# Where the spectra of modes 56 to 59 are made, and when the first output unit is prepared, in a fused attention and spectral-mixing kernel

## The chip, the cores and the metric

The kernel runs on one core of one Trainium2 chip. A core has five engines with instruction queues of their own: TensorE (PE, with its weight loads PEld), VectorE (DVE), ScalarE (ACT), GpSimd (POOL) and SyncE (SP). All of them work on on-chip memory (SBUF, and PSUM for the results of matmuls); 16 DMA engines move data. In this kernel SP issues the hardware-queued DMAs and POOL the software-queued ones. The metric is the device time of one execution in microseconds (us), as the median of several runs.

## The reference

There are two stages. The first is causal attention in a window of 128 tokens with a linear bias, for 8 batches, 8 heads, 576 tokens and 64 values a head. Its output, with the heads side by side, is `x`, of 8 x 576 x 512. The second mixes in frequency:

```
X = np.fft.rfft(x, axis=1)
Xr, Xi = (np.real(X[:, :n_modes]), np.imag(X[:, :n_modes]))
Yr = np.einsum('bmd,mde->bme', Xr, w_r) - np.einsum('bmd,mde->bme', Xi, w_i)
Yi = np.einsum('bmd,mde->bme', Xr, w_i) + np.einsum('bmd,mde->bme', Xi, w_r)
Y[:, :n_modes] = Yr + 1j * Yi
y = np.fft.irfft(Y, n=S, axis=1)
u = x + y
return (u + np.maximum(u @ w_ch, 0.0)).astype(np.float32)
```

There are 64 modes, and each has a real and an imaginary weight matrix of 512 x 512 in FP32, 1 MiB each: 127 of the 128 are needed (the imaginary part of mode 0 is not), 133 MB in all. The output is 9.44 MB.

## The kernel before

**Stages.** Attention runs until about 135 us of the span and leaves `x` in SBUF and the forward spectra of all batches in `XC`. Then comes the weight stage, until about 410 us, and then the output stage.

**The weight stage** (the loop over `g` at line 821) takes the weight matrices as 128 tiles in a fixed order, eight to a group of four modes: group `g` has modes 4g to 4g + 3, and `LAST` is 15. Within a group, `i` counts the places 0 to 7, and tile number `k` is 8g + i. In groups 0 to 14 two tiles are worked on together (at even `i`); in group 15 they come one by one, so that tile 120 is at `i` = 0 and tile 127 at `i` = 7. Four matmuls of 128x512 a tile (line 847) add it into `acc`, in which each mode of the group has 32 rows: 16 for the real parts of the batches and 16 for the imaginary ones. In group 15 the first three modes (60 to 62) are added into a second accumulator, `part_acc`.

Each tile is one DMA of 1 MiB that SP issues (line 465), once the tile whose buffer it takes is used up; some earlier ones are cast on the way, and POOL issues those. The last tile, 127, is loaded in three parts.

**Between the tiles** PE gets one piece of other work per `i`: first what stands in `quads` (a generator per group, resumed once per place), else the next entry of `side`, else a `warm()`: three matmuls of 128x512 whose result isn't used (line 664).

**From an accumulator to spectra.** `quad_end` scales `acc` into `yq` (DVE), transposes it (four PE transposes) and puts the result into `YT`, where the modes of 32 consecutive places (half `hf` 0 or 1) come together for each pair of batches (two DVE copies). When the 32 modes of a half are there, `spectra(hf, bp)` makes for the batch pair `bp`: four matmuls of 128x128 into `z`, which turn `YT` back into rows (one row for each batch, mode and real or imaginary part), and four of 128x512 with the channel weights `wch` into `zw`. ACT casts `zw` into `ZW[:, bp, hf]`, DVE `z` into `Z[:, bp, hf]`. The four blocks of half 0 are put into `side` after group 7. The four of half 1 (modes 32 to 63) are put there after group 13 and run in group 14, at `i` = 1 to 4: modes 56 to 63 are zero in `YT` then (line 541), and their rows in `Z` and `ZW` are filled later.

**The late modes.** `late_end` does this for group 14 (modes 56 to 59) and for the first three modes of group 15. It scales the accumulator into `yq` and has POOL copy the eight rows (six for the part) of each batch into `Z`, one DMA for each batch (`patch`, line 624): eight DMAs of 8 KB for group 14; six of 6 KB for the part, since batches 0 and 1 aren't copied there. It then transposes `yq`. For group 14 it also multiplies by `wch` (`late_channels`), casts on ACT, and has POOL copy the rows of each batch into `ZW`: eight more DMAs of 8 KB. Mode 63 is done after the loop (lines 911 to 946), and then the channel rows of the whole group 15.

**Output units.** There are 18 `units`, each of 64 or 128 tokens of two batches. During groups 8 to 14, `side` makes for each unit `project` (tokens times `wch`, plus half 0 from `ZW`, kept in `XW`) and `augment` (half 0 from `Z`, added into `x`). What is left for the output stage is half 1: a unit needs four small matmuls to bring `XW` into PSUM (`restore`, line 738), four with `ZW` (`spread`, line 635), and as many with `x` and `Z`. ACT then applies ReLU (line 778), DVE adds (line 802) and SP stores (lines 804, 811). For the first unit this is started inside the weight loop: at `i` = 7 of group 15, ahead of tile 127's matmuls, the pool `ps` of the weight stage is closed, the pool `head` is opened on its PSUM banks, and `begin(0)`, `channels(0)`, `take(0)`, `add_tokens(0)` and `finish_tokens(0)` issue 16 matmuls of 64x512. Units 0 and 1 take the modes 60 to 63 of batches 0 and 1 straight from `yq` and `yw`, through the table `FM` (`last_rows`, line 762).

**What sets the order.** The program runs in the order in which it is written (`manual_schedule`): each engine takes its own instructions in that order and waits by semaphores for what other engines and DMAs make. PSUM has eight banks of 128 x 512 FP32.

Of the kernel before, what the change touches and what calls it, by code (L numbers as in the profile page):

```python
# [10 lines left out]
FP32 = mybir.dt.float32  # L11
BF16 = mybir.dt.bfloat16
# [8 lines left out]
P = 128  # L21
# [378 lines left out]
def kernel(  # L400
# [10 lines left out]
    nc = tc.nc  # L411
    ctx.enter_context(tc.manual_schedule(engines=ALL | {SP}))
    B, H, S, _ = q.shape
    NM, DM, _ = moe_w_r.shape
# [3 lines left out]
    HM = NM // 2  # L418
# [21 lines left out]
    LAST = NM // 4 - 1  # L440
    turns = []
# [26 lines left out]
    with ExitStack() as actx:  # L468
        at = _Attention(tc, actx, q, k, v, (ident, F, FT), x, XC, raw)
        n = len(at.units)  # L470
# [67 lines left out]
    with ExitStack() as mctx:  # L538
        fix = mctx.enter_context(tc.tile_pool(name="fix", bufs=1))
        YT = fix.tile([P, 2, 4, B, HM, 2], BF16, name="YT")  # L540
        nc.gpsimd.memset(YT[:, 1, :, :, HM - 8 :], 0.0)
        pool = mctx.enter_context(tc.tile_pool(name="fin", bufs=2))
        wctx = mctx.enter_context(ExitStack())
        wpool = wctx.enter_context(tc.tile_pool(name="w", bufs=NWA, reuse_waits="tile"))
# [4 lines left out]
        ps = pctx.enter_context(tc.tile_pool(name="fps", bufs=1, space=PSUM))  # L549
        heads, free, idle = {}, [], []  # L550

        def late_end(acc, g, n):

            rows = slice(0, 32 * n)
            yq = pool.tile([P, DM], BF16, tag="yq", bufs=3)
            nc.vector.tensor_scalar_mul(yq[rows], acc[rows], 2.0 / S)
            patch([(nc.gpsimd, b) for b in range(2 if g == LAST else 0, B)],
                  yq, g, lambda b: Z[:, b // 2, 1], 0, 2 * n)
            yield
            tr = lps.tile([P, 4, P], BF16, tag="tr", name="tr")  # L560
            for et in range(4):
                nc.tensor.transpose(tr[:, et, rows], yq[rows, et * P : (et + 1) * P],
                                    ident[rows, rows])
            yT = pool.tile([P, 2, 4, P], BF16, tag="xT", name="xT")[:, 0]
            nc.vector.tensor_copy(yT[:, :, rows], tr[:, :, rows])
            heads[g] = yq, yT
            if n < 4:
                return
            yield
            zw = ps.tile([P, DM], FP32, tag="zw", bufs=1, name="zw")  # L570
            yw = pool.tile([P, DM], BF16, tag="yq", bufs=3)
            late_channels(zw, yT, yw, slice(0, DM))
            patch([(nc.gpsimd, b) for b in range(B)], yw, g, lambda b: ZW[:, b // 2, 1])

        def late_channels(zw, yT, yw, c):
            for et in range(4):
# [40 lines left out]
            zw = ps.tile([P, DM], FP32, tag="zw", bufs=1, name="zw")  # L617
            spectra(hf, bp, z, zw)

        def patch(todo, rows, g, dst, lo=0, hi=8):  # L620

            for queue, b in todo:
                r = 64 * (b % 2) + 8 * (g % 8)
                queue.dma_start(out=dst(b)[r + lo : r + hi],  # L624
                                in_=rows.rearrange("(k v) e -> k v e", v=16)[lo:hi, b])

# [190 lines left out]
        quads, side, recycle = [], [], list(again)  # L817
        ZW = Z = XW = FM = FC = pairs = wch = w2 = None
        K1 = spot[again[-1]]
        turn = iter(turns)  # L820
        for g in range(NM // 4):
            if g == 0:
                lps.tile([P, 2, 4, P], BF16, tag="tr", name="tr")
            acc = (lps if g % 2 else ps).tile([P, DM], FP32, tag="acc", bufs=1, name="acc")
            if g == LAST:
                part_acc = ps.tile([P, DM], FP32, tag="z", bufs=1, name="z")
            for i in range(8):
                k = 8 * g + i
                if i == 7 and g == LAST:
                    pctx.close()  # L830
                    head = mctx.enter_context(
                        tc.tile_pool(name="hps", bufs=1, space=PSUM, reuse_waits="tile"))
                    heads.update(mm=[head], yy=[head])
                    idle.append(0)
                    free.append(0)
                    begin(0)
                    channels(0)
                    take(0)
                    add_tokens(0)
                    finish_tokens(0)  # L840
                now = next(turn) if g == LAST or i % 2 == 0 else []
                for a in range(4):
                    for t in now:
                        m, ri = t // 2, t % 2
                        c0 = (a // 2 * 2 * NC + 16 * (1 - ri) + a % 2 * 8) * NM + m
                        into = part_acc if g == LAST and m < NM - 1 else acc
                        nc.tensor.matmul(  # L847
                            into[32 * (m % 4) : 32 * (m % 4) + 32],
                            lhsT=XC[:, c0 : c0 + 31 * NM + 1 : NM], rhs=wq[t][a],
                            start=(ri == 0 and a == 0), stop=(ri == (m > 0) and a == 3),  # L850
                            tile_position=(0, 32 * (m % 4)),
                        )
                own = next((t for t in homes if spot[t] == k), None)
                if own is None:
                    continue
                if recycle:
                    load_w(1, early, True, [recycle.pop(0)])
                elif homes[own] not in (early, None):
                    load_w(1, homes[own], False)
                if k == K1:  # L860
                    actx1.close()
                    w2 = mctx.enter_context(
                        tc.tile_pool(name="w2", bufs=NWB, side="right", reuse_waits="tile")
                    )
                    load_w(NWB, w2, False)
                    right = mctx.enter_context(
                        tc.tile_pool(name="late", bufs=1, side="right", reuse_waits="tile")
                    )
                    wch = right.tile([P, 4, DM], BF16, name="wch")
                    nc.gpsimd.dma_start(out=wch, in_=moe_w_ch.rearrange("(a p) e -> p a e", p=P))  # L870
                    ZW = right.tile([P, B // 2, 2, DM], BF16, name="ZW")
                    Z = right.tile([P, B // 2, 2, DM], BF16, name="Z")
                    XW = right.tile([P, len(units), 2, DM], BF16, name="XW")
                    FM = right.tile([P, 2, 2 * P], BF16, name="FM")
                    nc.gpsimd.memset(FM, 0.0)
                    for b in range(2):
                        nc.gpsimd.dma_start(
                            out=FM.rearrange("(k v) b s -> k v b s", v=16)[:, b, b],
                            in_=FT[64 * b + 56 : 64 * b + 64, b, : 2 * P],
                        )  # L880
                    FC = right.tile([P, P], BF16, name="FC")
                    pairs = right.tile([P, P], BF16, name="pairs")
                    nc.gpsimd.memset(FC, 0.0)
                    for i, rows in enumerate((slice(0, 64), slice(64, P))):
                        nc.gpsimd.tensor_copy(FC[rows, i::2], FT[rows, i, FULL * P :])
                        nc.gpsimd.tensor_copy(pairs[:, i::2], ident[:, rows])

                if quads:
                    if next(quads[0], True):
                        quads.pop(0)  # L890
                elif side and (i != 3 or g > LAST - 4):
                    side.pop(0)()
                elif g > LAST - 2 and k < 2 * NM - 1 or g == LAST - 2 and not side:
                    warm()
                if g == LAST and i == 5:
                    quads.append(late_end(part_acc, g, 3))
                    next(quads[0])
            if g < LAST:
                quads.append((late_end(acc, g, 4) if g == LAST - 1 else quad_end(acc, g)))
                next(quads[0])  # L900
            if g == 7:
                side += [partial(stream_spectra, 0, bp) for bp in range(B // 2)]
                for j in range(len(units)):
                    side += [partial(project, j), *([partial(augment, j - 1)] if j else [])]
                side.append(partial(augment, len(units) - 1))
            elif g == LAST - 2:
                side = [partial(stream_spectra, 1, bp) for bp in range(B // 2)] + side
        wctx.close()
        heads["out"] = mctx.enter_context(tc.tile_pool(name="res", bufs=6, reuse_waits="tile"))

# [8 lines left out]
        for i, c in enumerate(sides):  # L919
            nc.scalar.mul(yq[96:, c], acc[96:, c], 2.0 / S)  # L920
            for et in (2 * i, 2 * i + 1):
# [1 line left out]
                                    ident[96:, 96:])  # L923
            nc.vector.tensor_copy(yT[:, 2 * i : 2 * i + 2, 96:],
                                  trs[i][:, 2 * i : 2 * i + 2, 96:])
        patch([(nc.sync, 0), (nc.sync, 1)], yq, LAST, lambda b: Z[:, b // 2, 1])
        patch([(nc.sync, 2)] + [(nc.gpsimd, b) for b in (3, 4, 5, 6)], yq, LAST, lambda b: Z[:, b // 2, 1], 6)
        yw = F[:, : DM // (2 * NM)].rearrange("p a b -> p (a b)")
        for i, c in enumerate(sides):
            zl = zps.tile([P, DM], FP32, tag=f"z{i}", name=f"zl{i}")  # L930
# [10 lines left out]
        take(1)  # L941
        begin(1)
        channels(1)
        channel_rows = partial(patch, rows=yw, g=LAST, dst=lambda b: ZW[:, b // 2, 1])
        channel_rows([(nc.sync, 0), (nc.sync, 1)] + [(nc.gpsimd, b) for b in range(2, B)])
        patch([(nc.gpsimd, 7)], yq, LAST, lambda b: Z[:, b // 2, 1], 6)

        assert not side
        for j in (0, 1):
# [37 lines left out]
```

## Time and profile before

| | us |
|---|---|
| three runs | 445.92, 446.85, 446.88; median 446.85 |
| the profiled execution, whole time | 446.24 |
| its span, first to last instruction | 444.1 |
| busy in the span: PE / DVE / ACT / POOL | 329.6 / 184.4 / 162.6 / 59.5 |
| tile 120's matmuls start | 391.53 |
| tile 127's matmuls start | 409.66 |
| first matmul behind the loop (line 915) | 410.70 |
| first store issued | 415.37 |

Times inside the execution are counted from the start of the span. A line of the timeline has the start, the duration from the first to the last of the instructions that it merges, the engine, the line of the program, the operation, what it writes and reads, the shape and the number of instructions; in brackets stands how long the engine sat idle before it, and what ended that ("issue" is time in which it waited for nothing that the profile shows). SP's DMA issues are shown as SPq. A line of the table of stretches has the stretch, its length, the busy time of each engine in it, the granted TensorE clock (1.00 is full, 0.50 half), the busy share of the DMA engines, and what they moved.

### The profile page before, as it was taken

How to read it: one execution, taken by the hardware profiler on the slowest of the kernel's cores; microseconds unless marked ns; L12 is line 12 of the kernel's file. 1: busy time of each engine (PE TensorE's matmuls, PEld its weight loads, DVE VectorE, ACT ScalarE, POOL GpSimd, SP SyncE). 2: the span in 40 equal slices, each digit the busy share in tenths (PEclk: the TensorE clock that was granted, in tenths of full speed). 3: DMA queues.
4: the chain of work that ended last, by engine and by line, in shares of the span. 5: the costliest groups of instructions: out<-in, count | busy, mean ns of one | idle time of the engine just before them, and what ended most of it. 6: DMA issues, size and time to landing. Idle time of an engine off the chain costs nothing. (4 is left out here: it accounts for less than half of the span.)

```text
span 444.1 us, 8410 instructions
## 1 busy us (share of the span) xinstructions
PE 329.6 (74%) x3488; PEld 180.2 (41%) x3510; DVE 184.4 (42%) x331; ACT 162.6 (37%) x212; POOL 59.5 (13%) x123
## 2 busy tenths in 40 slices
PE   5579899979886554444455498998989998876982
PEld 3367677757664311111111133443444444332430
DVE  7789899987863201010000122232223322310684
ACT  6849899968860000000000012222222222210780
POOL 8611010101303100200000000000000000054500
PEclk9969999989998855555555579999999999999997
DMA  8999999999999999999999999999999999997598
GB/s 279 313 321 295 298 320 294 320 290 302 220 217 320 314 319 313 337 384 427 419 422 422 420 423 419 418 423 418 421 418 421 419 420 421 422 405 267 178 378 307
DMA packets 53721, 157.05 MB, mean 354 GB/s; under 512 B 5156, under 2 KB 24372, under 8 KB 41268
## 3 DMA queue, kind: packets, MB, share of 16 engines
q1 hardware_dynamic: 47860, 140.56, 82.0%
q0 software_dynamic: 5824, 15.97, 18.2%
q8 instruction: 27, 0.44, 0.4%
q14 instruction: 10, 0.08, 0.0%
HBM read 162.53 MB, written 9.44 MB: 387 GB/s over the span
## 5 line engine op out<-in xcount | busy, mean ns | idle before, releaser
L847 PE MATMUL acc<-w,XC 128*32 128x512 bf16 x456 | 92.7, 497 | 61.2 <-DMA w<-in_moe_w_r_dram 33.3
L847 PEld LDWEIGHTS <-XC 128*32 128x32 bf16 x508 | 39.5, 148 | 115.4 <-issue 101.7
L294 ACT ACTIVATE att<-sc 128x1024 bf16<-128x1024 f32 x64 | 64.1, 1032 | 10.2 <-PE sc L284 10.2
L612 ACT CAST ZW<-zw 128x512 bf16<-128x512 f32 x8 | 4.7, 586 | 134.6 <-PE zw L610 134.6
L331 PE MATMUL av<-vb,att 128*128 128x132 bf16 (+1 forms) x576 | 38.7, 218 | 10.9 <-DVE x L347 5.3
L331 PEld LDWEIGHTS <-att 128*128 128x128 bf16 x704 | 36.8, 99 | 16.3 <-DVE x L347 9.7
L678 PE MATMUL my<-wch,xT 128*64 128x512 bf16 x288 | 34.5, 381 | 5.8 <-ACT x L709 4.3
L584 DVE TENSOR_SCALAR yq<-acc 128x512 bf16<-128x512 f32 x13 | 8.9, 687 | 71.7 <-PE acc L847 71.7
L687 ACT CAST XW<-my 128x512 bf16<-128x512 f32 x36 | 19.3, 589 | 51.5 <-PE my L635 51.5
L624 POOL DMA_DIRECT2D Z<-yq x19 | 9.7, 519 | 209.2 <-issue 203.0
L659 DVE COPY xT<-tr 128x1024 bf16<-128x1024 bf16 x18 | 12.5, 692 | 55.6 <-PE tr L657 55.6
L256 ACT COPY qkT<-tp 128x1152 bf16<-128x1152 bf16 x30 | 33.5, 1116 | 2.8 <-PE tp L250 2.3
L284 PE MATMUL sc<-qkT 64*64 64x256 bf16 (+2 forms) x640 | 25.1, 263 | 4.9 <-ACT qkT L256 1.2
L347 DVE TENSOR_TENSOR x<-av,rec 128x640 bf16<-128x640 f32 x32 | 26.4, 824 | 1.1
L678 PEld LDWEIGHTS <-xT 128*64 128x64 bf16 x288 | 17.2, 109 | 21.7 <-issue 9.3
L802 DVE TENSOR_TENSOR o<-yy,r 128x1024 f32<-128x1024 f32 (+1 forms) x22 | 21.5, 1025 | 4.7 <-ACT r L778 3.0
L233 DVE CAST vb<-vr 64x1024 bf16<-64x1024 f32 x32 | 22.6, 708 | 0.6 <-DMA vr<-in_v_dram 0.4
L710 DVE CAST x<-my 128x512 bf16<-128x512 f32 x18 | 12.5, 692 | 24.6 <-PE my L635 24.6
L709 ACT CAST x<-my 128x512 bf16<-128x512 f32 x18 | 10.6, 586 | 32.3 <-PE my L635 32.3
L284 PEld LDWEIGHTS <-qkT 64*64 64x64 bf16 x640 | 14.5, 109 | 19.1 <-issue 16.1
L305 DVE TENSOR_TENSOR att<-att,mask 128x1024 bf16<-128x1024 bf16 x32 | 20.6, 684 | 0.0
L778 ACT ACTIVATE r<-mm 128x1024 f32<-128x1024 f32 (+1 forms) x22 | 17.9, 874 | 4.7 <-PE mm L748 2.5
(134 smaller groups left out, 401.2 us busy)
## 6 DMA issues: line engine op xcount, KB each, us to landing
w<-in_moe_w_i_dram SPq DMA_DIRECT2D x49, 1024.0 KB, 17.9
w<-in_moe_w_r_dram SPq DMA_DIRECT2D x48, 1024.0 KB, 16.4
qr<-in_q_dram SPq DMA_DIRECT2D x16, 576.0 KB, 9.3
kr<-in_k_dram SPq DMA_DIRECT2D x16, 576.0 KB, 8.0
vr<-in_v_dram SPq DMA_DIRECT2D x64, 128.0 KB, 7.6
out_dram<-o SPq DMA_DIRECT2D x13, 512.0 KB, 4.6
w<-in_moe_w_r_dram POOLq DMA_DIRECT2D x12, 512.0 KB, 8.9
w<-in_moe_w_i_dram POOLq DMA_DIRECT2D x10, 512.0 KB, 8.6
```

The source lines that it names most:

```text
L233: nc.vector.tensor_copy(self.vb[u % 2][row, :, :, :, W * half : W * half + D], src[row, :2])
L256: (self.nc.vector.tensor_copy if u < 2 and w == "q" else self.nc.scalar.copy)(dst.rearrange("q h (p j) -> q h p j", j=TPP), tp.rearrange(" ...
L284: nc.tensor.matmul(sc[64 * half : 64 * half + 64, e, j * 256 + c0 : j * 256 + c0 + n], lhsT=qkT[row, 1, h, k0 + j : k0 + P : 2], rhs=qkT[r ...
L294: self.nc.scalar.activation(self.att[u % 2][:, kt * 8 * P : (kt + 1) * 8 * P], sc.rearrange("p e n -> p (e n)"), AF.Exp, scale=1.0 / math. ...
L305: nc.vector.tensor_tensor(out=rows, in0=rows, in1=self.table[:, heads], op=ALU.mult)
L331: nc.tensor.matmul(bank[:, qt * W : qt * W + rhs[j].shape[1]], lhsT=att[:, o : o + P], rhs=rhs[j], start=(n == 0 and j == 0), stop=(n == l ...
L347: nc.vector.tensor_tensor(out=self.x[:, b, :, cs].rearrange("p t (h d) -> p h t d", h=2), in0=tiles[:, :, :, :D], in1=rec.unsqueeze(-1).br ...
L678: nc.tensor.matmul(mm[ROWS[half]], lhsT=lhsT, rhs=wch[:, dt], start=(dt == 0), stop=False, skip_group_check=True,)
L687: nc.scalar.copy(XW[:, j, n], mms[n])
L778: nc.scalar.activation(r[:, c], mm[:, c], AF.Relu)
L802: nc.vector.tensor_tensor(out=o[:, c], in0=yy[:, c], in1=r[:, c], op=ALU.add)
L847: nc.tensor.matmul(into[32 * (m % 4) : 32 * (m % 4) + 32], lhsT=XC[:, c0 : c0 + 31 * NM + 1 : NM], rhs=wq[t][a], start=(ri == 0 and a == 0 ...
```

## The change

Group 14 (modes 56 to 59) ends with `quad_end` like every group before it, so its rows reach `Z` and `ZW` through `YT` and `spectra`. Only modes 60 to 63 are zero in `YT`. The four `spectra` blocks of half 1 are therefore put into `side` one group later, after group 14, and run in group 15 at `i` = 1 to 4, behind the matmuls of tiles 121 to 124, where `late_channels` and fillers stood. In group 14 their places go to the two entries of `side` that are left, and to fillers. The branch for four modes in `late_end` is gone, with its sixteen row copies. Since `z` and `part_acc` now live at the same time, `part_acc` has a PSUM bank of its own. The first unit's 16 matmuls, with the closing and opening of the pools, are issued at `i` = 6, ahead of tile 126's matmuls, instead of at `i` = 7. The new way in which `now` is found gives the same tiles at the same places.

```diff
-        nc.gpsimd.memset(YT[:, 1, :, :, HM - 8 :], 0.0)
+        nc.gpsimd.memset(YT[:, 1, :, :, HM - 4 :], 0.0)
...
-        def late_end(acc, g, n):
-
-            rows = slice(0, 32 * n)
+        def late_end(acc):
+
+            rows = slice(0, 96)
             yq = pool.tile([P, DM], BF16, tag="yq", bufs=3)
             nc.vector.tensor_scalar_mul(yq[rows], acc[rows], 2.0 / S)
-            patch([(nc.gpsimd, b) for b in range(2 if g == LAST else 0, B)],
-                  yq, g, lambda b: Z[:, b // 2, 1], 0, 2 * n)
+            patch([(nc.gpsimd, b) for b in range(2, B)], yq, lambda b: Z[:, b // 2, 1], 0, 6)
             yield
...
-            heads[g] = yq, yT
-            if n < 4:
-                return
-            yield
-            zw = ps.tile([P, DM], FP32, tag="zw", bufs=1, name="zw")
-            yw = pool.tile([P, DM], BF16, tag="yq", bufs=3)
-            late_channels(zw, yT, yw, slice(0, DM))
-            patch([(nc.gpsimd, b) for b in range(B)], yw, g, lambda b: ZW[:, b // 2, 1])
+            heads[LAST] = yq, yT
...
             if g == LAST:
-                part_acc = ps.tile([P, DM], FP32, tag="z", bufs=1, name="z")
+                part_acc = ps.tile([P, DM], FP32, tag="pa", bufs=1, name="pa")
             for i in range(8):
                 k = 8 * g + i
-                if i == 7 and g == LAST:
+                if i == 6 and g == LAST:
                     pctx.close()
...
-                now = next(turn) if g == LAST or i % 2 == 0 else []
+                now = turns.pop(0) if turns and spot[turns[0][0]] == k else []
...
                 if g == LAST and i == 5:
-                    quads.append(late_end(part_acc, g, 3))
+                    quads.append(late_end(part_acc))
                     next(quads[0])
             if g < LAST:
-                quads.append((late_end(acc, g, 4) if g == LAST - 1 else quad_end(acc, g)))
+                quads.append(quad_end(acc, g))
                 next(quads[0])
...
-            elif g == LAST - 2:
-                side = [partial(stream_spectra, 1, bp) for bp in range(B // 2)] + side
+            elif g == LAST - 1:
+                assert not side
+                side = [partial(stream_spectra, 1, bp) for bp in range(B // 2)]
```

The calls of `patch` behind the loop lose the argument `g`, which was `LAST` there; they do the same as before.

More of the change, by code (lines that the diff above doesn't have):

```diff
@@ L618, in stream_spectra, with patch @@
             spectra(hf, bp, z, zw)
-        def patch(todo, rows, g, dst, lo=0, hi=8):
+        def patch(todo, rows, dst, lo=0, hi=8):
             for queue, b in todo:
-                r = 64 * (b % 2) + 8 * (g % 8)
+                r = 64 * (b % 2) + 8 * (LAST % 8)
                 queue.dma_start(out=dst(b)[r + lo : r + hi],
@@ L819 @@
         K1 = spot[again[-1]]
-        turn = iter(turns)
         for g in range(NM // 4):
@@ L925 @@
                                   trs[i][:, 2 * i : 2 * i + 2, 96:])
-        patch([(nc.sync, 0), (nc.sync, 1)], yq, LAST, lambda b: Z[:, b // 2, 1])
-        patch([(nc.sync, 2)] + [(nc.gpsimd, b) for b in (3, 4, 5, 6)], yq, LAST, lambda b: Z[:, b // 2, 1], 6)
+        patch([(nc.sync, 0), (nc.sync, 1)], yq, lambda b: Z[:, b // 2, 1])
+        patch([(nc.sync, 2)] + [(nc.gpsimd, b) for b in (3, 4, 5, 6)], yq, lambda b: Z[:, b // 2, 1], 6)
         yw = F[:, : DM // (2 * NM)].rearrange("p a b -> p (a b)")
@@ L943 @@
         channels(1)
-        channel_rows = partial(patch, rows=yw, g=LAST, dst=lambda b: ZW[:, b // 2, 1])
+        channel_rows = partial(patch, rows=yw, dst=lambda b: ZW[:, b // 2, 1])
         channel_rows([(nc.sync, 0), (nc.sync, 1)] + [(nc.gpsimd, b) for b in range(2, B)])
-        patch([(nc.gpsimd, 7)], yq, LAST, lambda b: Z[:, b // 2, 1], 6)
+        patch([(nc.gpsimd, 7)], yq, lambda b: Z[:, b // 2, 1], 6)
         assert not side
```

## The prediction

> **What bounds the kernel now.** I read four views in this order: the table of stretches (who is busy, how fast data comes), the timeline of the last eight weight tiles, POOL's own timeline, and the table again in pieces of 3.41 us for the TensorE clock. First the stretches; columns are the time, busy us of PE, PEld, DVE, ACT and POOL with their counts, granted clock, DMA share and GB/s:
>
> ```profile
> 370.00:395.69 25.69, 21.25 (x135) 9.12 (x138) 7.64 (x13) 6.06 (x11) 3.69 (x8) 1.00 1.01 420
> 395.69:407.39 11.70, 7.28 (x28) 2.97 (x28) 0.69 (x1) 0.00 (x0) 5.56 (x11) 1.00 1.00 357
> 407.39:409.00 1.61, 1.60 (x16) 0.83 (x19) 0.22 (x1) 0.00 (x0) 1.61 (x4) 1.00 0.50 178
> 409.00:409.50 0.50, 0.50 (x16) 0.14 (x8) 0.13 (x1) 0.00 (x0) 0.50 (x2) 1.00 0.18 35
> ```
>
> The weight stage is bound by the DMA engines (share 1.0), and at 420 GB/s; but while the last tiles come in, the engines are as full and move 357. The timeline names what else runs there:
>
> ```profile
> 391.53 1.12 PE L847 MATMUL z<-w,XC 128*32 128x512 bf16 x4
> 395.69 1.07 PE L847 MATMUL z<-w,XC 128*32 128x512 bf16 x4 [0.70 <-DMA w<-in_moe_w_r_dram]
> 398.58 1.07 PE L847 MATMUL z<-w,XC 128*32 128x512 bf16 x4 [1.06 <-DMA w<-in_moe_w_i_dram]
> 401.55 1.07 PE L847 MATMUL z<-w,XC 128*32 128x512 bf16 x4 [1.16 <-DMA w<-in_moe_w_r_dram]
> 404.45 1.07 PE L847 MATMUL z<-w,XC 128*32 128x512 bf16 x4 [1.07 <-DMA w<-in_moe_w_i_dram]
> 405.45 0.82 PE L664 MATMUL my<-wch,ident 128*128 128x512 bf16 x3
> 407.39 1.07 PE L847 MATMUL acc<-w,XC 128*32 128x512 bf16 x4 [1.13 <-DMA w<-in_moe_w_r_dram]
> 409.66 1.12 PE L847 MATMUL acc<-w,XC 128*32 128x512 bf16 x4
> 410.70 0.39 PE L915 MATMUL zl<-wch,ident 128*128 128x512 bf16 x1
> ```
> ```profile
> 392.00 4.19 POOL L624 DMA_DIRECT2D Z<-yq  x8 [202.99 <-issue]
> 397.53 1.04 POOL L624 DMA_DIRECT2D ZW<-yw  x2 [1.34 <-DMA Z<-yq]
> ...
> 401.38 1.11 POOL L624 DMA_DIRECT2D ZW<-yw  x2 [0.28 <-DMA Z<-yq]
> 406.54 3.03 POOL L624 DMA_DIRECT2D Z<-yq  x6 [4.04 <-DVE yq L556]
> ```
>
> See three things. Tiles 122 to 126 start at steps of 2.89, 2.97, 2.90 and 2.94 us, each released by a weight DMA; at 420 GB/s a tile of 1,048,576 bytes takes 2.50. The slow stretch is that in which the sixteen row copies of modes 56 to 59 are issued (392.0 to 402.5) and land (5.6 us later, in the table of DMA issues). And tile 127 has no DMA in its bracket: PE comes to it at 409.66 straight from other work, when 35 GB/s still trickles. From line 915 on, everything follows that tile, and the output ends at 444.1.
>
> **The change part by part.** I follow one number: when PE reaches line 915, now 410.70.
>
> **Removed: sixteen POOL DMAs of 8 KB** (8 to Z, 8 to ZW; 0.52 us of POOL each), with them one ACT cast of 0.59, one DVE copy of 0.42 and four matmuls of 0.81 together. POOL, ACT and DVE wait in this stretch, so these cost nothing by themselves. For the stream, the row is 11.70 us for four tiles against 4 x 2.50 = 9.99: the copies are the only other traffic, so 1.71 us, 0.107 a copy. Bounds: 0 (the stream is slow for another reason) to 1.71, plus 0.2 if tile 122 was already held up. I take 1.71, because the slow steps begin with the copies. Tile 126 then starts at 407.39 - 1.71 = 405.68, tile 125 at 403.18.
>
> **Kept: six Z copies of modes 60 to 62.** They are issued from 1.0 + 0.11 + 0.69 + 0.3 us after tile 125 starts (rows: 404.45, DVE 405.55 for 0.69, POOL 406.54), so 405.3 to 408.3, beside the last tile as before. Between 0 and 6 x 0.107 = 0.64 of extra; I take 0, since their place against the tiles is the same. POOL's next copies come after line 920, near 409.4: free.
>
> **Moved: four spectra blocks from group 14 to tiles 121 to 124.** Each issues 8 matmuls with 8 weight loads, an ACT cast of 0.59 and a DVE cast of 0.69, no DMA. On PE one runs 379.39 to 380.57 = 1.18 us; straight behind another one, with a wait of 0.37 for ACT's cast, 380.57 to 382.28 = 1.71. A tile's own matmuls take 1.00, so 2.18 of the 2.50 that a tile takes to come: hidden, PE waits 0.3 a tile. At 1.71 it is 2.71, and four tiles fall 0.84 behind; tile matmuls lie between the blocks here, so I take 1.18. What covers it is the DMA wait of 1.1 us now filled by three filler matmuls (0.82) and idle time. They move past eight weight issues of group 14 on SP, which wait for PE's tile matmuls; a weight lands 14 to 19 us after its issue, so SP has slack. Group 14's end makes two DVE copies of 0.30 to YT for one of 0.42: beside tile 121.
>
> **Moved: the first unit's 16 matmuls of 64 columns with 16 weight loads**, no DMA and no other queue, from between tiles 126 and 127 to ahead of 126. Now they run 408.67 to 409.65, 0.98 us on the path. Then they stand behind tile 125 (403.18 + 1.00 = 404.18) and the fillers (0.82): 405.00 to 405.98, 0.30 of it later than tile 126's arrival. Their banks could be those of modes 60 to 62, read by DVE until 404.18 + 0.11 + 0.69 = 404.98: no wait, at most 0.2. Queued behind is tile 126: 405.98 + 1.00 (407.39 to 408.39 now) = 406.98; four transposes, 0.28 (408.39 to 408.67), 407.26; tile 127, 1.04 (409.66 to 410.70): **408.30**. Its data: at 407.39 now, 178 x 1.61 + 35 x 0.50 = 0.30 MB are missing, and all is there by 409.5, so by 407.8 then; PE asks for the last quarter at 408.04. Late next is thus PE, by 0.2.
>
> **The bank and the memset.** The new tag "pa" is a bank more; the zeroed columns halve a POOL memset of 0.67 us at 135.6, with nothing waiting. 0.
>
> Sum: 410.70 - 408.30 = 2.40 us earlier; what follows is unchanged in work. The profiled execution took 446.24 (span 444.1 and 2.1 around it), so 443.84; the median of the three runs is 0.61 above it, 446.85, so **444.45** against that, and I say 444.4.
>
> **The clock, where a rule and a row differ.** Group 14 loses its spectra; three filler matmuls stand at five tiles (0.82 us in 2.5). Behind tile 117's pair PE is done near 385.6 and waits until 387.96 with one matmul of 0.25 between: a pause of 2.1 us. The clock rows:
>
> ```profile
> 135.13:138.54 3.41, 1.54 (x22) 1.36 (x24) 1.22 (x4) 0.55 (x2) 0.67 (x1) 1.00 1.04 305
> 138.54:141.96 3.42, 3.42 (x24) 1.55 (x26) 0.00 (x0) 0.00 (x0) 1.05 (x2) 0.50 1.03 323
> 258.01:261.42 3.41, 3.41 (x16) 1.18 (x12) 0.69 (x1) 0.46 (x1) 0.00 (x0) 0.50 1.02 423
> 261.42:264.83 3.41, 3.21 (x22) 1.57 (x21) 0.69 (x1) 0.80 (x2) 0.00 (x0) 1.00 1.01 420
> 397.95:401.36 3.41, 1.82 (x7) 0.74 (x7) 0.00 (x0) 0.00 (x0) 2.73 (x6) 1.00 1.03 366
> ```
>
> A piece 45% busy is followed by half clock, one 53% busy is not, and one full piece at half clock brings it back. A piece that holds the pause of 2.1 is 38% busy. Where the pieces lie changes from run to run, so a half-clock piece from about 388 is as likely as not. PE is then full (pair 2.1, fillers 2.6), so it lasts one piece and costs 3.41 / 2 = 1.71 us of work, against 0.9 us of idle time ahead of tile 121 and 0.3 at each of four more: 2.1. I charge nothing; the other end is that 1.2 of it stays.
>
> The Trainium skill, "TensorE: Matmul & The Clock Gate", in "HAM oscillation", warns only of PE-idle gaps above about 3.4 us; by it 2.1 us would be harmless and the clock stays up. The row at 135.13 contradicts it: its longest pause is 1.5 us and the clock fell. By the page the time is 444.4, by the rows 444.4 to 445.6.
>
> **The rivals.**
> - *The clock falls and part is left at the end.* For: the 45% row. Against: the full row, and the slack of 2.1. 0.5 to 1.7 us lost: 444.9 to 446.1.
> - *The stream does not recover; the copies were not its brake* (the change does half of what it says). For: the last tile also comes in parts, and 357 is an average. Against: share 1.0 at 420 up to the copies. Tile 126 stays at 407.39; the first unit fits the 1.13 us ahead of it; tile 127 starts at 408.67, its last quarter at 409.5 + 0.05, line 915 near 409.8: 0.9 gained, 445.9.
> - *PE becomes the bound of the last tiles: slower.* One mechanism: a spectra block takes S between tiles, and four tiles are late by 4 x (1.00 + S - 2.50). It eats the 2.40 at S = 2.1. Measured are 1.18 and 1.71; half clock gives 2.4 and tiles of 2.0, 1.9 us a tile, so two such tiles make 3.8 - 2.4 = +1.4: 448.2. Against: a full piece of 3.41 us returns the clock, and two tiles need 8.8.
>
> **How the numbers follow.** 0.2% (0.9 us) is about what a measurement can tell from no change. The forecast has 0.60, with its own range 443.9 (0.2 more from tile 122, and 0.3 from the first unit) to 445.3 (S = 1.71); the clock's remainder 0.15 (0.11 faster, 0.04 same); the stream 0.10 (half and half); PE-bound 0.11, all slower; 0.04 for no change that I can name. Faster 0.76, same 0.13, slower 0.11. The range 443.4 to 446.5 holds the first three; below it goes 0.4 for the scatter of the runs shown (0.96 us).
>
> **What would show it.** After: tiles 122 to 126 at steps near 2.50 and 420 GB/s there; no POOL copy between 392 and 404; sixteen matmuls ahead of tile 126; line 915 near 408.3, and the same 33.4 us from it to the end. Wrong if the steps stay at 2.9, if tiles 121 to 124 start without a DMA as releaser, or if the clock reads 0.50 after 392.

## The result, and the profile after

The changed kernel takes 444.28 us (median of 6 runs, 443.83 to 445.23) against 446.87 for the kernel before (6 runs, 445.92 to 448.13): a ratio of 0.9943, with a 95% interval of 0.9925 to 0.996. The profiled execution took 443.83 with a span of 441.7, 2.4 us less than the profiled one before.

The table of stretches of the changed kernel, with the columns of the one before (stretch, length, busy us of PE, PEld, DVE, ACT and POOL with counts, granted clock, DMA share, GB/s); the second row runs from tile 122 to tile 125:

```profile
370.00:395.58 25.58, 20.07 (x124) 8.49 (x122) 5.75 (x11) 3.43 (x7) 0.00 (x0) 1.00 1.01 421
395.58:403.11 7.53, 6.77 (x36) 3.20 (x36) 2.08 (x3) 1.75 (x4) 0.00 (x0) 1.00 1.01 415
...
404.00:405.00 1.00, 1.00 (x8) 0.35 (x11) 0.69 (x1) 0.00 (x0) 0.00 (x0) 1.00 0.87 338
405.00:406.00 1.00, 1.00 (x17) 0.39 (x12) 0.00 (x0) 0.00 (x0) 0.54 (x2) 1.00 0.61 238
406.00:407.00 1.00, 1.00 (x7) 0.41 (x7) 0.00 (x0) 0.00 (x0) 1.00 (x3) 1.00 0.38 139
407.00:408.00 1.00, 1.00 (x7) 0.55 (x7) 0.36 (x1) 0.00 (x0) 1.00 (x3) 1.00 0.21 62
```

And its timeline at the last tiles (line 838 holds the tile matmuls here, line 907 is the old line 915), with POOL's only work there:

```profile
393.10 1.07 PE L838 MATMUL pa<-w,XC 128*32 128x512 bf16 x4 [1.11 <-DMA w<-in_moe_w_i_dram]
395.58 1.06 PE L838 MATMUL pa<-w,XC 128*32 128x512 bf16 x4 [0.23 <-DMA w<-in_moe_w_r_dram]
398.06 1.07 PE L838 MATMUL pa<-w,XC 128*32 128x512 bf16 x4 [0.23 <-DMA w<-in_moe_w_i_dram]
400.63 1.07 PE L838 MATMUL pa<-w,XC 128*32 128x512 bf16 x4 [0.31 <-DMA w<-in_moe_w_r_dram]
403.11 1.06 PE L838 MATMUL pa<-w,XC 128*32 128x512 bf16 x4 [0.23 <-DMA w<-in_moe_w_i_dram]
...
405.85 1.12 PE L838 MATMUL acc<-w,XC 128*32 128x512 bf16 x4
...
408.30 0.39 PE L838 MATMUL acc<-w,XC 128*32 128x512 bf16 x1 [0.20 <-DMA w<-in_moe_w_i_dram]
408.62 0.39 PE L907 MATMUL zl<-wch,ident 128*128 128x512 bf16 x1
```
```profile
405.46 3.02 POOL L616 DMA_DIRECT2D Z<-yq  x6 [216.25 <-issue]
```

Three things answer to the lines of before. Tiles 122 to 125 now come at steps of 2.48, 2.48, 2.57 and 2.48 us, where they were 2.9, and the stretch moves 415 GB/s where it moved 357. Tile 126 has no DMA in its bracket: PE comes to it from the first unit's matmuls. And tile 127's last quarter has one: PE waited 0.20 us for it, while the DMA share runs down from 0.87 to 0.21. Line 907 starts at 408.62, 2.08 us earlier than line 915 did.

From one execution to the next the end of the weight stage lies earlier or later, by 2 us between kernels that are the same up to there: the first of the two points below lies anywhere from 387.64 to 390.11 us in the fourteen profiles. So below I count from the start of the main part of group 14's last pair of matmuls (seven of its eight, released by a DMA, here before and after) to line 907 or 915. Call it M.

```profile
387.96 1.07 PE L847 MATMUL acc<-w,XC 128*32 128x512 bf16 x7 [1.24 <-DMA w<-in_moe_w_i_dram]
```
```profile
388.11 1.09 PE L838 MATMUL acc<-w,XC 128*32 128x512 bf16 x7 [2.10 <-DMA w<-in_moe_w_i_dram]
```

| kernel | M, us | ratio of the times to before, 95% interval |
|---|---|---|
| before | 22.74 | 1 |
| changed | 20.51 | 0.9943 (0.9925 to 0.996) |
| copies gone, unit in its old place | 20.85 | 0.9963 (0.9947 to 0.9979) |
| unit moved only | 22.80 | 0.9992 (0.9976 to 1.0008) |
| before without the sixteen copies | 20.79 | 0.9953 (0.9935 to 0.9971) |
| changed, sixteen copies put back | 21.54 | 0.997 (0.9957 to 0.9983) |
| changed, one copy of the same bytes | 20.74 | 0.9961 (0.9941 to 0.9981) |
| changed, no fillers in group 14 | 20.70 | 0.997 (0.9951 to 0.9989) |
| changed, more filler at tiles 121 to 124 | 22.11 | 0.9984 (0.9963 to 1.0005) |
| changed, rows of modes 60 to 62 later | 20.41 | 0.9948 (0.9931 to 0.9966) |
| changed, last tile in halves | 20.61 | 0.9967 (0.9954 to 0.998) |
| three edits together | 20.64 | 0.995 (0.9933 to 0.9968) |
| changed once more | 20.43 | 0.9948 (0.9928 to 0.9967) |
| sixteen copies on ScalarE's queue | 26.24 | 1.0068 (1.0046 to 1.0091) |

In three of these (halves, changed once more, ScalarE's queue) the record of line 907 is missing from the trace; there I take ACT's first scaling behind the loop, less the 0.11 us by which it stands behind line 907 in the kernels where both are recorded.

### The profile page after: what moved, and what is told of

The parts are those of the page before. It is cut to its first block, busy times and chain, and to the rows that moved or that the text cites. A ratio compares the mean times of both kernels' runs of the same rounds, so it can differ in the third digit from the quotient of the medians.

```text
span 441.7 us, 8410 instructions
## 1 busy us (share of the span) xinstructions
PE 332.8 (75%) x3509; PEld 179.9 (41%) x3509; DVE 184.5 (42%) x332; ACT 162.1 (37%) x211; POOL 50.2 (11%) x107
## 5 line engine op out<-in xcount | busy, mean ns | idle before, releaser
L616 POOL DMA_DIRECT2D Z<-yq x11 | 5.5, 511 | 217.4 <-issue 216.2
L271 PE MATMUL sc<-bias,ident 128*128 128x512 bf16 x64 | 20.8, 409 | 1.3 <-ACT att L294 1.3
(130 smaller groups left out, 396.6 us busy)
```

The costliest lines, as they stand in the source:

```text
L271: nc.tensor.matmul(sc[:, e], lhsT=self.ident, rhs=self.bias[:, hv].rearrange("p j n -> p (j n)"), start=True, stop=False, skip_group_check ...
```

## The experiments

**Theory**: the sixteen small row copies braked the weight stream, and that is most of the gain; moving the unit's matmuls off the way to tile 127 is the rest. **Rivals**: the stream's end is slow by itself and the unit's place is the gain; PE or its clock is near to being the bound.

### One part alone: the copies

```diff
-                if i == 6 and g == LAST:
+                if i == 7 and g == LAST:
```

> The changed kernel with the first unit's 16 matmuls back between tiles 126 and 127. Theory (the sixteen row copies brake the weight stream): tiles 122 to 126 come at steps of 2.50 us; tile 126 starts near 405.6, ends 406.6, transposes to 406.9, the unit to 407.9, tile 127 to 408.95, where line 907 starts: 1.75 us before the kernel before, 0.3 behind the changed one; about 444.7 us. Rival (the gain comes from the unit's place): line 907 near 410, about 446.

Measured: steps of 2.49, 2.49, 2.60, 2.49 and 2.49 us; M 20.85, 1.89 less than before and 0.34 more than the changed kernel. Counted by M, all of it is as the theory had it. The time itself, 445.75, is 1.1 above the number; in the profiled execution that lies ahead of the last tiles (M's first point is at 389.68, 1.6 later than in the changed kernel), and for the others no profile tells.

```profile
407.22 1.07 PE L838 MATMUL acc<-w,XC 128*32 128x512 bf16 x4 [0.67 <-DMA w<-in_moe_w_r_dram]
409.48 1.12 PE L838 MATMUL acc<-w,XC 128*32 128x512 bf16 x4
410.53 0.39 PE L907 MATMUL zl<-wch,ident 128*128 128x512 bf16 x1
```

In these lines tile 126 waits for its data again, and the unit's matmuls stand between the two tiles.

### The other part alone: the unit's place

```diff
-                part_acc = ps.tile([P, DM], FP32, tag="z", bufs=1, name="z")
+                part_acc = ps.tile([P, DM], FP32, tag="pa", bufs=1, name="pa")
...
-                if i == 7 and g == LAST:
+                if i == 6 and g == LAST:
```

> The kernel before with only the unit's 16 matmuls moved ahead of tile 126 (and the bank of its own for modes 60 to 62); row copies and spectra as before. Theory: steps stay at 2.9 us, tile 126 starts at 407.4, tile 127 at 408.67, line 915 near 409.8, 0.9 earlier than before: about 446.0. Rival (the unit's place is the gain): 444.5.

Measured: steps of 2.97, 2.92 and 2.89, M 22.80, ratio 0.9992. The rival is out: the move alone brings nothing that can be seen. But I had given it 0.9 us. The lines show where that went:

```profile
408.81 1.12 PE L847 MATMUL acc<-w,XC 128*32 128x512 bf16 x4
...
411.33 0.39 PE L847 MATMUL acc<-w,XC 128*32 128x512 bf16 x1 [0.30 <-DMA w<-in_moe_w_i_dram]
411.65 0.39 PE L915 MATMUL zl<-wch,ident 128*128 128x512 bf16 x1
```

PE is at tile 127 early and then waits for its last quarter. That landed 0.5 us later behind the last pair than in the profile before (last weight packet at 21.95 against 21.40 us, by the trace's DMA packets). In this profile the stream was late ahead of the copies already: tile 121's load is complete 6.08 us behind the start of the last pair, 4.92 before, and tile 122's 8.39 against 7.69, when the copies' packets have hardly begun (396.6). So that half microsecond looks like scatter between executions. The other 0.4 was an error of mine: in the kernel before, the last load is complete at 409.82, which would put line 915 near 410.2 at the earliest, not at 409.8. The interval of the times allows up to 1.1 us of gain.

### The suspected cause taken out of the kernel before

The sixteen copies are left out, so modes 56 to 59 are missing from the output; fillers, late channels and spectra stay where they were.

```diff
-            patch([(nc.gpsimd, b) for b in range(2 if g == LAST else 0, B)],
-                  yq, g, lambda b: Z[:, b // 2, 1], 0, 2 * n)
+            if g == LAST:
+                patch([(nc.gpsimd, b) for b in range(2, B)], yq, g, lambda b: Z[:, b // 2, 1], 0, 2 * n)
...
-            patch([(nc.gpsimd, b) for b in range(B)], yw, g, lambda b: ZW[:, b // 2, 1])
```

> The kernel before without the sixteen row copies of modes 56 to 59 (those modes are left out of the output); everything else in its place, fillers and late channels too. Theory: steps of 2.50 us, tile 126 near 405.7, line 915 near 409.0, 1.7 earlier: about 445.1. Rival (the end of the stream is slow by itself): steps stay at 2.9, 410.7, 446.9.

```profile
396.12 1.07 PE L846 MATMUL z<-w,XC 128*32 128x512 bf16 x4 [0.50 <-DMA w<-in_moe_w_r_dram]
398.61 1.07 PE L846 MATMUL z<-w,XC 128*32 128x512 bf16 x4 [0.66 <-DMA w<-in_moe_w_i_dram]
401.09 1.06 PE L846 MATMUL z<-w,XC 128*32 128x512 bf16 x4 [0.66 <-DMA w<-in_moe_w_r_dram]
403.57 1.06 PE L846 MATMUL z<-w,XC 128*32 128x512 bf16 x4 [0.67 <-DMA w<-in_moe_w_i_dram]
406.07 1.06 PE L846 MATMUL acc<-w,XC 128*32 128x512 bf16 x4 [0.67 <-DMA w<-in_moe_w_r_dram]
```

Measured: steps of 2.49, 2.48, 2.48 and 2.50; M 20.79; 445.07 us, where the theory had 445.1. Nothing but the copies was taken away, so they are what made the steps 2.9.

### The suspected cause put back into the changed kernel

Sixteen copies of eight rows of 1 KB go to an unused tile `SC`, eight at group 14's end and eight behind the first spectra block.

```diff
+        def scratch(yq, half):
+
+            for b in range(B):
+                r = 64 * half + 8 * b
+                nc.gpsimd.dma_start(out=SC[0][r : r + 8],
+                                    in_=yq.rearrange("(k v) e -> k v e", v=16)[:8, b])
```

> The changed kernel with sixteen copies of eight rows of 1 KB from POOL into an unused tile, issued where the removed ones were. Theory: the steps are 2.9 us again, tile 126 starts near 407.3, line 907 near 409.8, 1.2 us later than in the changed kernel: about 445.5. Rival (the slow steps had another cause): as the changed kernel, 444.3.

```profile
397.31 1.07 PE L850 MATMUL pa<-w,XC 128*32 128x512 bf16 x4
400.27 1.07 PE L850 MATMUL pa<-w,XC 128*32 128x512 bf16 x4 [0.70 <-DMA w<-in_moe_w_i_dram]
403.08 1.07 PE L850 MATMUL pa<-w,XC 128*32 128x512 bf16 x4 [0.55 <-DMA w<-in_moe_w_r_dram]
405.82 1.06 PE L850 MATMUL pa<-w,XC 128*32 128x512 bf16 x4 [0.48 <-DMA w<-in_moe_w_i_dram]
```

Steps of 2.96, 2.81 and 2.74, M 1.03 more, 445.6 us. The brake is back, about half as strong as in the kernel before (1.03 against the 1.9 that taking it away brought). The rows go to other partitions here, and the first copies are issued 2.3 us behind the start of the last pair instead of 4.0; which of the two it is, or scatter, no run tells. The granted clock fell to 0.50 for a piece here too (391.00 to 394.41, shown below), but that isn't the 1.03: it fell beside the same tiles in the run with the last tile in halves (from 389.93), and there tile 125 starts 14.92 us behind the last pair, against 16.16 here and 15.00 in the changed kernel.

### Bytes or number of copies

```diff
             nc.vector.tensor_scalar_mul(yq, acc, 2.0 / S if g else norm)
+            if g == LAST - 1:
+                nc.gpsimd.dma_start(out=SC[0], in_=yq)
```

> The changed kernel with one POOL copy of 128 rows of 1 KB into an unused tile at group 14's end: the bytes of the sixteen copies in one DMA. Counted from the start of group 14's last pair of tiles to line 907, which is 22.7 us in the kernel before, 20.5 in the changed one and 21.5 with sixteen copies put back. Theory A (each small DMA has its price, whatever it carries): 20.6, one weight step of 2.6. Theory B (the price goes by the 1 KB packets): 21.5 or more, steps of 2.9 while it lands.

```profile
395.10 1.07 PE L840 MATMUL pa<-w,XC 128*32 128x512 bf16 x4 [1.09 <-DMA w<-in_moe_w_i_dram]
398.13 1.07 PE L840 MATMUL pa<-w,XC 128*32 128x512 bf16 x4 [0.77 <-DMA w<-in_moe_w_r_dram]
400.46 1.07 PE L840 MATMUL pa<-w,XC 128*32 128x512 bf16 x4
402.94 1.07 PE L840 MATMUL pa<-w,XC 128*32 128x512 bf16 x4 [0.22 <-DMA w<-in_moe_w_r_dram]
```

The same 128 KB in one copy of 128 rows make one step 3.03 us and the rest short again; M is 20.74, 0.23 more than in the changed kernel. At 420 GB/s the bytes alone are 0.31. So the bytes are not what sixteen copies cost (1.03 put back, 1.9 to 1.95 taken away). But the run doesn't tell theory A from theory B. By the DMA packets in the trace, the sixteen copies are 128 packets of 1 KB and 384 of 4 bytes, and the one copy is 32 packets of 4 KB and 16 of 4 bytes: its rows didn't travel as packets of 1 KB. Whether the price goes by the number of DMAs or of packets stays open. The Trainium skill, in "DMA: Bandwidth & Descriptors", section "Bandwidth", states that transfers under 64 KB are dominated by their descriptors; the sixteen were of 8 KB and the one of 128 KB. That is about a transfer's own rate; what small transfers take from another stream is measured here and not stated there.

### PE's clock

The fillers of group 14 are left out.

```diff
-                elif g > LAST - 2 and k < 2 * NM - 1 or g == LAST - 2 and not side:
+                elif g > LAST - 1 and k < 2 * NM - 1 or g == LAST - 2 and not side:
```

> The changed kernel without the filler matmuls of group 14. Pauses of 3.9 us between its pairs, pieces of 3.41 us under 35% busy. Theory: the granted clock falls to 0.50 in group 14, PE is then full with tile 120, 121 and the first spectra at half speed, and the clock is back within one or two pieces; up to 1.7 us of work is lost and 2.1 of slack takes it up: 20.5 to 21.3 us from the last pair to line 907, time within 0.8 of the changed kernel. Rival (the clock stays low and PE becomes the bound): over 23, slower than before.

The table of stretches of this run, in the pieces of 3.41 us in which the clock changes:

```profile
382.29:385.70 3.41, 1.07 (x7) 0.59 (x7) 0.13 (x1) 0.00 (x0) 0.00 (x0) 1.00 1.02 423
...
389.11:392.53 3.42, 2.80 (x10) 0.84 (x6) 0.69 (x1) 0.00 (x0) 0.00 (x0) 0.50 1.01 422
392.53:395.94 3.41, 2.87 (x18) 1.29 (x16) 1.17 (x3) 0.00 (x0) 0.00 (x0) 0.99 1.02 423
```

A piece 31% busy brings half clock, for two pieces, until one was 82% busy. Tiles 120 and 121 take longer, tile 122 waits for its data again, and M is 20.70: 0.19 us lost. The ratio of the times, 0.9951 to 0.9989, overlaps the changed kernel's. The clock rival is real, and at the last tiles it costs next to nothing.

That the clock can fall even with the fillers, as the prediction had it, shows in the run with the copies put back, whose pieces fell otherwise, beside the changed kernel's own:

```profile
387.59:391.00 3.41, 1.34 (x9) 0.74 (x9) 0.24 (x1) 0.00 (x0) 0.00 (x0) 1.00 1.02 423
391.00:394.41 3.41, 3.41 (x10) 0.94 (x7) 0.45 (x1) 0.00 (x0) 2.40 (x5) 0.50 1.02 423
```
```profile
384.32:387.74 3.42, 1.68 (x7) 0.61 (x6) 0.00 (x0) 0.00 (x0) 0.00 (x0) 1.00 1.00 417
387.74:391.15 3.41, 3.04 (x16) 1.45 (x16) 0.69 (x1) 0.00 (x0) 0.00 (x0) 1.00 1.02 423
```

The pause of 2.1 us lies whole in the first piece (39% busy): half clock for one piece. In the changed kernel's profile it was split, 49% busy, and the clock stayed. Ten of the profiles have this pause. In the three where a piece holds it whole (copies put back, more filler, halves) and in one where a piece holds 1.85 us of it (ScalarE's queue), that piece is 38 to 45% busy and the clock fell; in the six where it is split between two pieces, the clock stayed.

### How much room PE has

```diff
                     side.pop(0)()
+                    if g == LAST:
+                        warm()
```

> The changed kernel with three filler matmuls (0.66 to 0.82 us) behind each of the four spectra blocks. Theory (PE has 0.3 us to spare a tile): each tile takes 2.9 on PE against 2.5 to arrive, tiles 122 to 125 start 0.4 later each, line 907 is 1.3 to 1.8 later than in the changed kernel (21.8 to 22.3 from the last pair), about 445.8. Rival (PE has more room than the rows say): 20.5, 444.3.

```profile
397.66 1.12 PE L838 MATMUL pa<-w,XC 128*32 128x512 bf16 x4
400.54 1.12 PE L838 MATMUL pa<-w,XC 128*32 128x512 bf16 x4
403.43 1.12 PE L838 MATMUL pa<-w,XC 128*32 128x512 bf16 x4
406.32 1.12 PE L838 MATMUL pa<-w,XC 128*32 128x512 bf16 x4
```

No tile waits for a DMA any more, the steps are 2.88, 2.89 and 2.89, and M is 22.11, 1.60 more: inside the expected 21.8 to 22.3. The time is 446.42, nearly all of the gain gone. Not all of the 1.60 is the fillers': the clock also fell here, at 390.5 for one piece, and tile 121, which is ahead of them, starts 5.40 us behind the last pair instead of 4.99. PE, which no longer waits, can't make that 0.41 good, so I estimate the fillers' share at 1.2, a little under the expected 1.3. This is the slower rival of the prediction at work: with 0.7 us more a tile PE is the bound.

### The last tile

By the DMA packets, the last MiB of weights takes 4.25 us to land in the changed kernel (4.28 before), where a MiB further ahead in the stream takes 2.5. I took that for a slow last tile, and three runs went after it. But a count of bytes mixes tiles. The counter that tells of a load's completion rises in 16 steps, and the trace has the time of each: in the changed kernel those of tile 126 go from 402.17 to 405.57, and those of tile 127's last part from 404.77 to 408.26. Tile 127 is thus complete 2.69 us behind tile 126 (2.47 before, 2.47 to 2.87 in the fourteen profiles), and tiles 122 to 126 follow one another at 2.48 to 2.56. The last tile is hardly slower than any other. What is drawn out is each load: its steps lie 3.4 us apart in all.

```diff
-            patch([(nc.gpsimd, b) for b in range(2, B)], yq, lambda b: Z[:, b // 2, 1], 0, 6)
...
-        patch([(nc.sync, 2)] + [(nc.gpsimd, b) for b in (3, 4, 5, 6)], yq, lambda b: Z[:, b // 2, 1], 6)
+        patch([(nc.sync, 2)] + [(nc.gpsimd, b) for b in (3, 4, 5, 6)], yq, lambda b: Z[:, b // 2, 1])
...
-        patch([(nc.gpsimd, 7)], yq, lambda b: Z[:, b // 2, 1], 6)
+        patch([(nc.gpsimd, 7)], yq, lambda b: Z[:, b // 2, 1])
```

> The changed kernel without the six copies of modes 60 to 62 beside the last tile: their rows go with mode 63's, in the same DMAs behind the loop (eight rows instead of two). Theory (these copies brake the last tile too): its last part lands 0.6 us sooner, PE is then the bound, line 907 comes 0.3 earlier (20.2 from the last pair), about 444.0. Rival (the last tile is slow because of its small parts): its landing still takes 4.2 us behind tile 126's, 20.5, 444.3. If the wider rows are late in the output stage instead: up to 0.5 later.

Measured: 4.11 us instead of 4.25, M 20.41; tile 127 is complete 2.58 us behind tile 126 instead of 2.69. The landing hardly moved: these six copies brake little or nothing.

```diff
-                             else (slice(0, 2), slice(2, 3), slice(3, 4))):
+                             else (slice(0, 2), slice(2, 4))):
```

> The changed kernel with tile 127 loaded in two halves of 512 KB instead of 512, 256 and 256 KB. In every run so far its last bytes come 4.1 to 5.6 us behind tile 126's, where a whole tile takes 2.5. Theory (the 2 KB rows of the quarters and their small packets are the brake): 3.3 to 3.7 us, the last half is there 0.5 us sooner, PE has two matmuls left then instead of one; line 907 at 20.1 to 20.4 us from the last pair instead of 20.5, time 444.0. Rival (the engines run dry unevenly at the stream's end, whatever the parts): 4.2 stays, and line 907 is 0.25 later for the second matmul.

Measured: 4.38 us, M 20.61, and 2.67 us from tile 126 to tile 127: the rival. The small parts change nothing either, and PE has two matmuls left behind the landing.

The third has both edits, and `k < 2 * NM - 3` in the condition of the fillers, which leaves out the one ahead of the unit:

> The changed kernel with three edits together: tile 127 in two halves, the rows of modes 60 to 62 with mode 63's behind the loop, and no filler between tile 125 and the first unit. The filler stands ahead of the unit's 16 matmuls on PE (0.75 us); without it tile 126 starts at its landing and PE is at tile 127 0.4 sooner. Theory: line 907 at 19.7 to 20.2 us from the last pair, 0.3 to 0.8 less than the changed kernel; about 443.8. Rival (the last landing sets the end): 20.4, 444.2.

```profile
406.02 1.07 PE L837 MATMUL acc<-w,XC 128*32 128x512 bf16 x4 [0.45 <-DMA w<-in_moe_w_r_dram]
407.30 0.67 PE L837 MATMUL acc<-w,XC 128*32 128x512 bf16 x2
408.52 0.61 PE L837 MATMUL acc<-w,XC 128*32 128x512 bf16 x2 [0.56 <-DMA w<-in_moe_w_i_dram]
409.06 0.39 PE L906 MATMUL zl<-wch,ident 128*128 128x512 bf16 x1
```

PE now waits for tile 126 and again, 0.56 us, for the last half: M 20.64, the last MiB in 3.91, tile 127 complete 2.50 us behind tile 126. The landing sets the end, as the rival said, and the three edits together are worth nothing beside the changed kernel on the same chip:

> The changed kernel once more, on the chip of these runs, as their measure: 20.5 us from the last pair to line 907, ratio to the kernel before near 0.9945.

That gave 0.9948 and M 20.43, against 0.995 and 20.64. So no version here beats the changed kernel. The share of the DMA engines that runs down at the end (0.87, 0.61, 0.38, 0.21 in the four last microseconds) fits 16 engines of which some are about 3.4 us ahead of others: those ahead run out first, and the ones behind set each tile's landing. The distances between the 16 steps are the same within 0.02 us for tiles 125 and 126. Where the stream had run short ahead of the last tiles (the next run), the steps of tile 126 lie only 0.62 us apart. The trace doesn't name the engine of a step, so this reading is not shown; and why engines would be so far apart stays open.

### The same copies on another queue

```diff
-                nc.gpsimd.dma_start(out=SC[0][r : r + 8],
+                nc.scalar.dma_start(out=SC[0][r : r + 8],
```

> The changed kernel with the same sixteen unused copies issued by ScalarE, a hardware queue, instead of POOL. Theory (any second queue with small copies brakes the weight stream): steps near 2.9 us while they land, 21.3 to 22.2 us from the last pair to line 907. Rival (the price belongs to POOL's software queue): steps of 2.5 to 2.6, 20.6 to 20.9. ScalarE's casts of ZW stand behind its issues, at most 0.6 us each; if that holds the spectra up, tiles 121 to 124 start without a DMA as their releaser.

It doesn't answer its question. M is 26.24 and the time 449.79, 2.6 us slower than before, but the table of SP's waits tells of something else:

```profile
SPq L465 <- DMA w<-in_moe_w_i_dram: 16.1, 1, 16.1
SPq L465 <- DMA SC<-yq: 7.3, 3, 6.7
```

In the trace, SP's weight loads and ScalarE's copies count up the same eight completion counters (semaphores 100 to 104 and 107 to 109), and SP's loads of 392.63, 393.24, 400.29 and 401.07 go out 0.06 us after the DMA before them on their counter is complete. For the first of them that is SP's own load of 376.13, for the other three one of the copies. Weight loads that go out between 379 and 393 us in the kernel before went out between 392 and 406 here: SP waited, first 16.1 us for an older weight load and then 7.3 for these copies, and the stream ran short. Whether copies from a hardware queue brake a full stream as POOL's do was not tried without this, and the packets give no clear hint: with these copies landing beside a full stream, weight packets of 8 KB took 309 ns in the median from 397 to 399 and from 404 to 406 us, but 335 and 349 in the two microseconds from 406 to 408.

## Why the prediction was right, point by point

- *The sixteen copies cost the stream 1.71 us.* Right in kind, shown from both sides: without them (unit unmoved) M falls by 1.89 and, from the kernel before, by 1.95; put back, it rises by 1.03. Tile 126's data was there by tile 126's turn, and tile 125 started at 403.11 where 403.18 was predicted. The price of 0.107 a copy is one for copies of this shape in this place: put back, with their rows in other partitions, they cost 0.064 each, and one copy of all the bytes cost 0.23. The trace's 8 KB weight packets show where the time went: each took 312 ns in the median until 396 us in the kernel before, 344 to 366 in the three-microsecond pieces from 396 to 408, and 312 throughout in the changed kernel.
- *The spectra blocks hide in the waits of tiles 121 to 124.* Right: 394.09 to 395.28 is 1.19 us (1.18 predicted), and each next tile was released by a DMA after 0.2 to 0.3 us of waiting (0.3 predicted). The run with more filler shows where that cover ends.
- *The unit's matmuls go ahead of tile 126 and delay it by 0.3.* Tile 126 started at 405.85; 405.98 was predicted. Their worth was 0.34 with the copies gone, and not to be seen with them there. The price of 0.9 that the prediction's second rival gave the move alone was wrong: it took the last quarter to be there 0.05 us after 409.5, and that load is complete only at 409.82.
- *Late next is PE, by 0.2.* Wrong. The last quarter's landing was: PE waited 0.20 for it, and line 907 started at 408.62, 0.32 later than the 408.30 of the sum. I had moved the table's trickle of before by the 1.71 that the earlier tiles gained, to 407.8; by the DMA packets the last weight byte was written at 407.74, but the load's counter was full only at 408.26, and the matmul started at 408.30. Half a microsecond lies between the last packet and the released matmul (0.47 to 0.56 in the eight profiles in which that matmul waits), and the sum had nothing for it.
- *What follows line 907 is unchanged.* 33.1 us to the end of the span instead of 33.4; from the first store to the end the fourteen profiles scatter from 28.4 to 29.1, so this 0.3 is no effect of the change. It made good the 0.32 above: that 443.83 was measured where the sum gave 443.84 is luck, closer than its terms.
- *The clock.* By the rows it could fall in group 14 and cost nothing. Both were seen: with the fillers in place it fell for one piece in the run with the last tile in halves (389.93 to 393.35), and tile 125 still started 14.92 us behind the last pair, 15.00 in the changed kernel. Without fillers it fell for two pieces and 0.19 us were lost. It does cost where PE has no room, as with more filler. The rule of the Trainium skill's "TensorE: Matmul & The Clock Gate" ("HAM oscillation", gaps above about 3.4 us) was too mild for this kernel: a pause of 2.1 was enough where it lay whole in one piece. Its Part 1, by which the window runs freely and doesn't start with the kernel, fits what the runs show: the same pause brought the clock down in four profiles and not in six, by where it lay in the pieces.

## What to carry to other kernels

In a stretch that the DMA engines bound, count every small copy that lands in it as part of the stream: copies of eight rows of 1 KB beside full weight loads cost 0.06 to 0.12 us each here, though POOL, which issued them, had nothing else to do, and one copy of all their bytes cost no more than its bytes. Engines that wait there (PE had 0.3 to 1.1 us a tile) can do the same work instead, as long as their time a tile stays under the tile's arrival. And when the bound is lifted, look for the next one in the completion of the last load, not in the mean rate: it came half a microsecond behind the last byte here. Measure a tile from completion to completion, since bytes of neighbouring tiles land mixed.

## What was not expected of the hardware

- The 16 completion steps of one weight load lie 3.0 to 4.9 us apart in all at the end of a full stream (tile 126, thirteen profiles), longer than the 2.5 us from tile to tile. So by bytes the last MiB takes 3.9 to 5.6 us, with the DMA share falling from 0.87 to 0.21, though tile 127 is complete 2.5 to 2.7 us behind tile 126.
- From 256 us on, the clock stayed up behind pieces 50% busy and more and fell behind pieces 46% busy and less. Busy share alone is no rule, though: in the changed kernel it fell behind one 50% busy (135.11 to 138.52); with the copies put back it stayed up behind one 44% busy (111.11 to 114.52), and at half clock it didn't come back behind one 85% busy (233.99 to 237.40). So the 45% and 53% of the prediction are two rows and no limits.
- Copies on ScalarE's hardware queue held up SP's weight loads by 16.1 and 7.3 us through the completion counters that the two share in this program.
